# Attention with beacon keys into soft MoE: score banks of the next pair ahead of the extras, the turned dispatch weights two batches behind

## The chip, the cores and the metric

One core of one Trainium2 chip runs the whole program. The metric is the device time of one execution in microseconds, lower is better.

## The reference

Attention over 8 batches, 8 heads, 576 queries, width 64, with 16 beacon keys ahead of the 576 causal ones; its output, as 4608 tokens of width 512, goes into a soft mixture of 8 experts with 4 slots each. `a` is the attention weight matrix, `d` the dispatch weights (normalized over tokens), `c` the combine weights (normalized over slots).

```python
scores = scale * np.matmul(q, k_all.transpose(0, 1, 3, 2))      # causal mask, softmax -> a
attn = np.matmul(a, v_all)                                      # [8, 8, 576, 64]
x = attn.transpose(0, 2, 1, 3).reshape(4608, 512)
logits = x @ phi                                                # 32 slots
d = np.exp(logits - logits.max(0)); d /= d.sum(0) + 1e-09
slot_input = (d.T @ x).reshape(8, 4, 512)
for e in range(8):
    slot_out[e] = np.maximum(slot_input[e] @ w1[e], 0.0) @ w2[e]  # w1 512x1024, w2 1024x512
c = np.exp(logits - logits.max(1)); c /= c.sum(1) + 1e-09
out = c @ slot_out.reshape(32, 512)
```

## The kernel before

The order of the instructions on each engine (PE, DVE, ACT, POOL, and SP, which issues transfers) is the order of the Python calls. The work goes in 32 pairs of heads, n = 4b + g for batch b and g = 0 to 3; the main loop runs n = 2 to 31 and is one pair deep in a pipeline: iteration n makes the scores of pair n and the A.V product of pair n-1.

The steps that the loop calls, with the lines of the profile:

- `scores(n, bank)`: a quarter of pair n's causal scores, as PE matmuls (L517) into one of two PSUM score buffers ("sc"), the exponential of it on ACT (L522) into `expT` (two buffers, by pair), and the causal mask on POOL (L508). Bank 0 has 992 elements per partition, bank 1 928, bank 2 768, bank 3 640. A score buffer is free when its exponential has read it.
- `transposes(m, which)`: the k or q of two pairs turned on PE in two pieces (L486) and copied out by DVE (L498). In even iterations it is k, in odd ones q, always ahead of its use.
- `attend(n, hh)`: A.V of one head of the pair (L538), with a column of ones for the softmax sums; one PSUM buffer ("av") holds both heads.
- `normalize(n)`: DVE adds an epsilon to the sums (L549), inverts them (L551) and multiplies (L552) into the batch's `x`.
- `x_transposes(n)`: the pair's part of `x` turned (L564) and copied to `xT` by DVE (L571).

Once per batch there are four extras:

- `logits(b)`: `xT` times phi (L583), then its exponential on ACT (L589) into `dT`, each of the 32 slots four times over, 640 elements. The last batch does it in two steps (L592 on ACT for 160 elements, L593 on DVE for the three copies).
- `dispatch(b)`: `dT` against `x` (L622), the slot sums (L600), and their addition into `acc` on DVE (L633, L636).
- `combine_T(b)`: `dT` turned on PE (L644) and copied into `eT` by DVE (L647), for the output at the end.
- `cast_v` and `perm_v`: the next batch's values, cast on POOL (L390, L394), permuted on PE (L404) into one score buffer and two "tr" buffers, and copied out by ACT (L407) and DVE (L410).

The "tr" PSUM buffers are two. Each piece of the k or q transposes, each `x_transposes`, `logits`, `dispatch`, `combine_T`, and two pieces of `perm_v` take one in turn, so that each waits until the one before the last has been copied out. `x` has two buffers, so batch b writes where batch b-2 was; `dT` has one.

The weights (33.5 MB in f32) come in over the POOL queue in pieces of 512 KB of f16 (`load_weights`, L449 and L456), paced by the loop: none or one piece an iteration, then two from batch 6 on. The last ones are `wt`, of experts 6 and 7. q, k and v come in over the SP queue (L351, L365, L377, L381) up to two batches ahead.

After the loop come the last pair, the last batch's logits and dispatch, the two expert products (`first`, L823; `second`, L838), a normalization (L860), and the output: combine matmuls (L909), scaling on ACT and DVE (L914, L916) and 13 transfers (L920). `fill` (L658) is a matmul on constants whose result nobody reads.

Of the kernel before, what the change touches and what calls it, by code (L numbers as in the profile page):

```python
# [14 lines left out]
AF = mybir.ActivationFunctionType  # L15
# [253 lines left out]
def kernel(  # L269
# [12 lines left out]
    nc = tc.nc  # L282
    P = 128
    B, H, S, D = q.shape
    Nb = beacon_k.shape[2]
    E, Dm, F = moe_w1.shape
    NSL = moe_phi.shape[1]
# [5 lines left out]
    NC5 = 5  # L293
# [45 lines left out]
    def head(n, hh):  # L339

        g = n % NG
        return 2 * g + hh if n >= NPAIR - 2 else 4 * (g // 2) + 2 * hh + g % 2
# [126 lines left out]
    def transposes(m, which):  # L469

        b, hb = divmod(m, 2)
        t = st["kq"[which], b, hb]
        if which == 1:
            qTs[m] = work.tile([P, 2, S], BF, name="qT", tag="qT")
            dst = qTs[m][:, :, :]
        else:
            if m:
                beacon_keys(m)
            dst = kTs[m % 2][:, :, Nb:Nb + S]
        for j0, j1 in ((0, 5), (5, NJ)):  # L480
            tp = ps_tr.tile([P, j1 - j0, P], BF, name="trps", tag="tr")
            for j in range(j0, j1):
                for hh in range(2):
                    lo, hi = 64 * hh, 64 * hh + 64
                    if m < 2 * B - 1:
                        nc.tensor.transpose(tp[lo:hi, j - j0, :],  # L486
                                            t[:, hh, j, :].bitcast(BF)[:, 1::2], idb[:, :])
                        continue
                    for u in range(2):
                        nc.tensor.transpose(tp[lo:hi, j - j0, 64 * u:64 * u + 64],  # L490
                                            t[lo:hi, u, j, :].bitcast(BF)[:, 1::2],
                                            idb[lo:hi, lo:hi])
            do = dst.rearrange("p u (s j) -> p u s j", j=NJ)[:, :, :, j0:j1]
            ti = tp[:, :, :].rearrange("p j (u s) -> p u s j", u=2)
            if j0 and (m == 0 or m == 1 and which):
                nc.scalar.activation(do, ti, AF.Copy)
            else:
                nc.vector.tensor_copy(out=do, in_=ti)  # L498
# [12 lines left out]
    def scores(n, bank, masked=True):  # L511
        base, w, mms = BANKS[bank]
        sc = ps_sc.tile([P, 2, 512], FP, name="sc", tag="sc")
        for (c, q0, qw, col) in mms:
            for hh in range(2):
                po = 64 * hh
                nc.tensor.matmul(sc[:, hh, col:col + qw],  # L517
                                 kTs[n // 2 % 2][po:po + D, n % 2, c * P:(c + 1) * P],
                                 qTs[n // 2][po:po + D, n % 2, q0:q0 + qw], start=True,
                                 stop=True)  # L520
        ex = exps[n % 2]
        nc.scalar.activation(ex[:, :, base:base + w], sc[:, :, 0:w], AF.Exp, scale=scale)  # L522
        if masked:
            select(n, bank)
# [3 lines left out]
    def attend(n, hh):  # L528
        b, g = divmod(n, NG)
        h = head(n, hh)  # L530
        if hh == 0:
            pool, tag = (ps_av, "av") if n < NPAIR - 1 else (ps_sc, "sc")
            avs[n] = pool.tile([P, 2, 512], FP, name="av", tag=tag)
        av = avs[n][:, hh, 0:NC5 * DD].rearrange("p (i d) -> p i d", d=DD)
        for i in range(NC5):
            for c in range(i + 1):
                o = BLK[c, i]
                nc.tensor.matmul(av[:, i, :], exps[n % 2][0:KW[c], hh, o:o + P],  # L538
                                 vhs[b % 2][0:KW[c], c, h, :],
                                 start=(c == 0), stop=(c == i))  # L540
# [17 lines left out]
    dTs = {}  # L558

    def x_transposes(n):  # L560
        b, t = divmod(n, NG)
        tp = ps_tr.tile([P, S], F16, name="xtps", tag="tr")
        for i in range(NC5):
            nc.tensor.transpose(tp[:, QLO[i]:QLO[i] + QW[i]],  # L564
                                xs[b][0:QW[i], i, 2 * t:2 * t + 2, :].rearrange(
                                    "p h d -> p (h d)"),
                                idh[0:QW[i], 0:QW[i]])
        if n == NPAIR - 2:
            nc.scalar.activation(xT[:, t, 0:S], tp[:, :], AF.Copy)
        else:  # L570
            nc.vector.tensor_copy(out=xT[:, t, 0:S], in_=tp[:, :])  # L571
# [3 lines left out]
    def logits(b, t0=0, t1=NDC):  # L575

        if t0 == 0:
            lps[b] = ps_tr.tile([P, NC5, NSL], FP, name="lgps", tag="tr")
            dTs[b] = work.tile([P, NC5, 4, NSL], F16, name="dT", tag="dT", bufs=1)
        lp = lps[b]  # L580
        for i in range(NC5):
            for t in range(t0, t1):
                nc.tensor.matmul(lp[:, i, :], xT[:, t, QLO[i]:QLO[i] + P],  # L583
                                 phih[:, t, :], start=(i == 0 and t == 0),
                                 stop=(i == NC5 - 1 and t == NDC - 1))
        if t1 < NDC:
            return
        if t0 == 0:
            nc.scalar.activation(dTs[b][:, :, :, :],  # L589
                                 lp[:, :, :].unsqueeze(2).broadcast_to([P, NC5, 4, NSL]), AF.Exp)  # L590
        else:
            nc.scalar.activation(dTs[b][:, :, 0, :], lp[:, :, :], AF.Exp)  # L592
            nc.vector.tensor_copy(  # L593
                out=dTs[b][:, :, 1:4, :],
                in_=dTs[b][:, :, 0:1, :].broadcast_to([P, NC5, 3, NSL]))

    def slot_sums(b, sp, into):
        for i in range(NC5):
# [40 lines left out]
    def combine_T(b):  # L639

        dT = dTs[b]
        tp = ps_tr.tile([P, S], F16, name="etps", tag="tr")
        for i in range(NC5):
            nc.tensor.transpose(tp[:, QLO[i]:QLO[i] + QW[i]],  # L644
                                dT[0:QW[i], i, :, :].rearrange("p g s -> p (g s)"),
                                idh[0:QW[i], 0:QW[i]])
        nc.vector.tensor_copy(out=eT[:, b * S:(b + 1) * S], in_=tp[:, :])  # L647
# [5 lines left out]
    def fill(count, late=True):  # L653

        pool, tag = (ps_tr, "tr") if late else (ps_av, "av")
        ps = pool.tile([P, 512], FP, name="fill", tag=tag)
        for _ in range(count):
            nc.tensor.matmul(ps[:, :], onesh[:, :], eT[:, 0:512], start=True, stop=True)  # L658
# [14 lines left out]
    with tc.manual_schedule(engines={ET.PE, ET.DVE, ET.Activation, ET.Pool, ET.SP}):  # L673
# [3 lines left out]
                          in_=beacon_k.rearrange("b h n d -> (b h) (n d)"))  # L677
# [44 lines left out]
        for c in range(4):  # L722
            for t in range(4):
                nc.vector.tensor_copy(
                    out=sel[32 * c:32 * c + 32, t, :].rearrange(
                        "p (m t) -> p m t", t=4)[:, :, t],
                    in_=idh[32 * c:32 * c + 32, 32 * c:32 * c + 32])
# [22 lines left out]
        load_v(2)  # L750
        load_qk(2, 0)

        for n in range(2, NPAIR):
            b, g = divmod(n, NG)
            scores(n, 0)
            scores(n, 1)
            if n // 2 + 1 < 2 * B:
                transposes(n // 2 + 1, n % 2)
            attend(n - 1, 0)
            scores(n, 2)  # L760
            if n >= 3:
                x_transposes(n - 3)
            attend(n - 1, 1)
            if n >= 7 and g == 3:
                combine_T(b - 1)
            normalize(n - 1)
            scores(n, 3)
            if n == NPAIR - 1:
                x_transposes(n - 2)
            if b and g == 2:  # L770
                logits(b - 1)
            if n >= 8 and g == 0:
                dispatch(b - 2)
            if b + 1 < B and g:
                parts = ((0,), (1,), (2,))[g - 1] if b else ((0,), (1, 2))[g - 2]
                for c in parts:
                    cast_v(b + 1, c)
                if g == 3:
                    perm_v(b + 1)
            if b + 2 < B:  # L780
                if g == 0:
                    load_v(b + 2)
                    load_qk(b + 2, 0)
                if g == 2:
                    load_bv(b + 2)
                    load_vr(b + 2)
                    load_qk(b + 2, 1)
            if n == 5:
                nc.vector.tensor_copy(out=phih[:, :, :], in_=phif[:, :, :])
            load_weights((0, 1, 1, 1)[g] if b < 6 else 2)  # L790
# [6 lines left out]
        n = NPAIR  # L797
# [3 lines left out]
        normalize(n - 1)  # L801
        x_transposes(n - 2)
        dispatch(B - 2)
        fill(2)
        x_transposes(n - 1)
        logits(B - 1, 0, NDC - 1)
        logits(B - 1, NDC - 1, NDC)
# [3 lines left out]
            out=sz1[:, :].rearrange("p (t e s) -> p t e s", t=NDC, s=SPE), in_=sizv)  # L811
# [148 lines left out]
```

## Time and profile before

| | |
|---|---|
| three runs | 201.41, 202.38, 203.35 us; median 202.38 |
| profiled execution | 200.63 us, its span 198.9 us, mean granted clock 0.956 |
| busy PE / DVE / ACT / POOL | 162.4 / 132.4 / 134.0 / 114.8 us |
| exponentials of scores (L522) | 128, 104.8 us |
| matmuls of scores (L517) and of A.V (L538) | 576 and 960, 43.7 and 40.3 us |
| DMA moved | 55.90 MB, 281 GB/s over the span |

The first 22 us fill the pipeline, the loop runs to about 153 us, the experts to 169 us, and the output to the end. PE is the busiest engine by its own time, but busy time is an average over all of these; the DMA rows give the share of the core's 16 DMA engines in use. A form such as `128x640` is partitions by elements. Times in the timeline count from the start of the span.

### The profile page before, as it was taken

How to read it: one execution, taken by the hardware profiler on the slowest of the kernel's cores; microseconds unless marked ns; L12 is line 12 of the kernel's file. 1: busy time of each engine (PE TensorE's matmuls, PEld its weight loads, DVE VectorE, ACT ScalarE, POOL GpSimd, SP SyncE). 2: the span in 40 equal slices, each digit the busy share in tenths (PEclk: the TensorE clock that was granted, in tenths of full speed). 3: DMA queues.
4: the chain of work that ended last, by engine and by line, in shares of the span. 5: the costliest groups of instructions: out<-in, count | busy, mean ns of one | idle time of the engine just before them, and what ended most of it. 6: DMA issues, size and time to landing. Idle time of an engine off the chain costs nothing.

```text
span 198.9 us, 7368 instructions
## 1 busy us (share of the span) xinstructions
PE 162.4 (82%) x3122; PEld 107.9 (54%) x3122; DVE 132.4 (67%) x279; ACT 134.0 (67%) x172; POOL 114.8 (58%) x264
## 2 busy tenths in 40 slices
PE   6798893889898898988989898898978999875200
PEld 2443561667586576756757665675856844542000
DVE  0352684678888888888789778788855532898300
ACT  2356694688888889888888788888787140783200
POOL 6049087359659847955965786799776400890000
PEclk9999999699999999999999999999999999997855
DMA  6999999999999999999999999999999995599991
GB/s 203 258 240 367 283 357 326 264 377 316 280 242 379 279 258 326 319 258 292 381 249 270 363 305 269 257 229 211 216 211 214 214 213 95 211 410 415 409 403 69
DMA packets 29845, 55.90 MB, mean 281 GB/s; under 512 B 7244, under 2 KB 15660, under 8 KB 29804
## 3 DMA queue, kind: packets, MB, share of 16 engines
q1 hardware_dynamic: 24764, 37.98, 56.0%
q0 software_dynamic: 4752, 16.78, 42.3%
q10 hardware_dynamic: 288, 0.59, 1.0%
q8 instruction: 26, 0.43, 0.8%
q14 instruction: 15, 0.12, 0.2%
HBM read 62.69 MB, written 9.44 MB: 363 GB/s over the span
## 4 chain that ended last, share of the span: by engine, by line


## 5 line engine op out<-in xcount | busy, mean ns | idle before, releaser
L522 ACT ACTIVATE expT<-sc 128x992 f16<-128x992 f32 (+3 forms) x128 | 104.8, 867 | 20.3 <-PE sc L517 19.7
L508 POOL TENSOR_SCALAR_AFFINE_SELECT expT<-expT 128x224 f16<-128x224 f16 (+3 forms) x128 | 55.1, 441 | 39.6 <-ACT expT L522 38.7
L517 PE MATMUL sc<-qT,kT 64*128 64x80 bf16 (+4 forms) x576 | 43.7, 246 | 11.2 <-ACT expT L522 5.4
L538 PE MATMUL av<-vh,expT 128*128 128x65 f16 (+1 forms) x960 | 40.3, 195 | 0.2 <-DVE x L552 0.2
L538 PEld LDWEIGHTS <-expT 128*128 128x128 f16 (+1 forms) x960 | 33.6, 98 | 4.3 <-POOL expT L508 0.8
L498 DVE COPY kT<-trps 128x640 bf16<-128x640 bf16 (+1 forms) x31 | 22.7, 773 | 19.6 <-PE trps L486 19.1
L517 PEld LDWEIGHTS <-kT 64*128 64x128 bf16 x576 | 17.1, 95 | 28.2 <-issue 22.4
L498 DVE COPY qT<-trps 128x640 bf16<-128x640 bf16 (+1 forms) x30 | 22.0, 773 | 8.4 <-PE trps L486 6.6
L552 DVE TENSOR_TENSOR x<-av,r 128x640 f16<-128x640 f32 x32 | 26.4, 824 | 1.1
L390 POOL CAST vc<-vstag 128x512 f16<-128x512 f32 x32 | 18.7, 614 | 1.6 <-ACT expT L522 1.6
L571 DVE COPY xT<-xtps 128x576 f16<-128x576 f16 x31 | 14.1, 456 | 6.0 <-PE xtps L564 5.8
L914 ACT ACTIVATE osb<-fps,rc 128x512 f32<-128x512 f32 (+1 forms) x18 | 11.2, 675 | 10.2 <-PE fps L909 9.5
L564 PE MATMUL xtps<-idh,x 128*128 128x128 f16 (+2 forms) x160 | 14.3, 217 | 0.4 <-issue 0.2
L916 DVE TENSOR_SCALAR osb<-fps,rc 128x512 f32<-128x512 f32 (+1 forms) x19 | 12.8, 727 | 1.3 <-PE fps L909 1.2
L658 PE MATMUL fill<-eT,onesh 128*128 128x512 f16 x36 | 11.6, 451 | 1.7 <-POOL onesh L691 1.5
L407 ACT ACTIVATE vh<-vps 128x1024 f16<-128x1024 f32 x8 | 8.2, 1027 | 6.6 <-PE vpt L404 6.6
L410 DVE CAST vh<-vpt 128x512 f16<-128x512 f32 x16 | 10.3, 684 | 3.6 <-PE vpt L404 3.6
L564 PEld LDWEIGHTS <-x 128*128 128x128 f16 (+2 forms) x160 | 9.2, 98 | 6.0 <-issue 5.5
L909 PE MATMUL fps<-so,eT 128*128 128x512 f16 (+1 forms) x37 | 11.2, 431 | 1.2 <-DVE so L860 0.8
L465 POOL COPY kT<-bkA 64x32 bf16<-64x32 bf16 x32 | 7.4, 232 | 7.9 <-DVE bkA L719 7.0
L486 PE MATMUL trps<-idb,kstag 128*64 128x128 bf16 x270 | 11.7, 234 | 0.1
L486 PE MATMUL trps<-idb,qstag 128*64 128x128 bf16 x270 | 10.9, 222 | 0.7 <-DVE vh L410 0.4
(98 smaller groups left out, 187.6 us busy)
## 6 DMA issues: line engine op xcount, KB each, us to landing
kstag<-in_k_dram SPq DMA_DIRECT2D x15, 576.0 KB, 10.0
qstag<-in_q_dram SPq DMA_DIRECT2D x15, 576.0 KB, 13.6
out_dram<-osb SPq DMA_DIRECT2D x11, 768.0 KB, 7.2
vstag<-in_v_dram SPq DMA_DIRECT2D x7, 1024.0 KB, 14.8
w1h<-in_moe_w_dram POOLq DMA_DIRECT2D x10, 512.0 KB, 8.6
w2h<-in_moe_w_dram POOLq DMA_DIRECT2D x10, 512.0 KB, 8.4
wt<-in_moe_w_dram POOLq DMA_DIRECT2D x7, 512.0 KB, 12.2
wv<-in_moe_w_dram POOLq DMA_DIRECT2D x4, 512.0 KB, 11.6
```

Of the source, the lines that this page charges most:

```text
L390: nc.gpsimd.tensor_copy(out=st["c", b][:, :, hs, :].rearrange("p t h d -> p h t d"), in_=st["v", b][:, hs, :, :])
L486: nc.tensor.transpose(tp[lo:hi, j - j0, :], t[:, hh, j, :].bitcast(BF)[:, 1::2], idb[:, :])
L498: nc.vector.tensor_copy(out=do, in_=ti)
L508: nc.gpsimd.affine_select(out=ap, in_=ap, compare_op=AL.is_ge, fill=0.0, base=cbase, pattern=pat, channel_multiplier=-1)
L517: nc.tensor.matmul(sc[:, hh, col:col + qw], kTs[n // 2 % 2][po:po + D, n % 2, c * P:(c + 1) * P], qTs[n // 2][po:po + D, n % 2, q0:q0 + qw ...
L522: nc.scalar.activation(ex[:, :, base:base + w], sc[:, :, 0:w], AF.Exp, scale=scale)
L538: nc.tensor.matmul(av[:, i, :], exps[n % 2][0:KW[c], hh, o:o + P], vhs[b % 2][0:KW[c], c, h, :], start=(c == 0), stop=(c == i))
L552: nc.vector.tensor_tensor(out=xs[b][:, :, head(n, 0):head(n, 1) + 1:head(n, 1) - head(n, 0), :].rearrange("p i h d -> p h i d"), in0=av[:, ...
L564: nc.tensor.transpose(tp[:, QLO[i]:QLO[i] + QW[i]], xs[b][0:QW[i], i, 2 * t:2 * t + 2, :].rearrange("p h d -> p (h d)"), idh[0:QW[i], 0:QW ...
L571: nc.vector.tensor_copy(out=xT[:, t, 0:S], in_=tp[:, :])
L658: nc.tensor.matmul(ps[:, :], onesh[:, :], eT[:, 0:512], start=True, stop=True)
L916: nc.vector.tensor_scalar(out=ou, in0=f[:, 0:hw], scalar1=rc[:, bb, j:j + 1], scalar2=None, op0=AL.mult)
```

## The change

Five things change, all in the order of calls but for one:

1. The exponential of the logits is always done in two steps: ACT writes 160 elements and DVE makes the three copies.
2. `scores(n + 1, 0)` is called in iteration n, after `normalize(n - 1)` and ahead of that iteration's extra, and `scores(2, 0)` ahead of the loop.
3. `scores(n, 2)` is called ahead of `attend(n - 1, 0)`, and `scores(n, 3)` ahead of `attend(n - 1, 1)`.
4. `combine_T` of batch b-2 is called at g = 0 after the normalization (it was that of batch b-1 at g = 3, ahead of the normalization), and that of batch 6 in the tail, where it takes the place of two fills.
5. `dispatch` of batch b-2 is called at g = 1 (it was g = 0).

The expression for the parts of `cast_v` is written in another way and gives the same parts.

```diff
@@ logits
-        if t0 == 0:
-            nc.scalar.activation(dTs[b][:, :, :, :],
-                                 lp[:, :, :].unsqueeze(2).broadcast_to([P, NC5, 4, NSL]), AF.Exp)
-        else:
-            nc.scalar.activation(dTs[b][:, :, 0, :], lp[:, :, :], AF.Exp)
-            nc.vector.tensor_copy(
-                out=dTs[b][:, :, 1:4, :],
-                in_=dTs[b][:, :, 0:1, :].broadcast_to([P, NC5, 3, NSL]))
+        nc.scalar.activation(dTs[b][:, :, 0, :], lp[:, :, :], AF.Exp)
+        nc.vector.tensor_copy(
+            out=dTs[b][:, :, 1:4, :],
+            in_=dTs[b][:, :, 0:1, :].broadcast_to([P, NC5, 3, NSL]))
@@ the main loop
+        scores(2, 0)
         for n in range(2, NPAIR):
             b, g = divmod(n, NG)
-            scores(n, 0)
             scores(n, 1)
             if n // 2 + 1 < 2 * B:
                 transposes(n // 2 + 1, n % 2)
+            scores(n, 2)
             attend(n - 1, 0)
-            scores(n, 2)
             if n >= 3:
                 x_transposes(n - 3)
+            scores(n, 3)
             attend(n - 1, 1)
-            if n >= 7 and g == 3:
-                combine_T(b - 1)
             normalize(n - 1)
-            scores(n, 3)
             if n == NPAIR - 1:
                 x_transposes(n - 2)
+            else:
+                scores(n + 1, 0)
+
+            if b > 1 and g == 0:
+                combine_T(b - 2)
+            if b > 1 and g == 1:
+                dispatch(b - 2)
             if b and g == 2:
                 logits(b - 1)
-            if n >= 8 and g == 0:
-                dispatch(b - 2)
             if b + 1 < B and g:
-                parts = ((0,), (1,), (2,))[g - 1] if b else ((0,), (1, 2))[g - 2]
-                for c in parts:
+                for c in ((g - 1,) if b else ((), (0,), (1, 2))[g - 1]):
                     cast_v(b + 1, c)
                 if g == 3:
                     perm_v(b + 1)
@@ the tail
         dispatch(B - 2)
-        fill(2)
+        combine_T(B - 2)
         x_transposes(n - 1)
```

## The prediction

> **What bounds the kernel now.** I read the page's DMA rows first, then the busy times by stretch, then the landing of the last weights, then one pair of heads in the timeline.
>
> ```profile
> DMA  6999999999999999999999999999999995599991
> ```
>
> ```profile
> core 0: us, PE busy (x) PEld busy (x) DVE busy (x) ACT busy (x) POOL busy (x), PEclk, DMA share, GB/s
> 62.00:79.00 17.00, 15.88 (x355) 11.40 (x356) 14.36 (x30) 14.56 (x19) 12.22 (x29) 1.00 1.07 300
> 135.00:152.00 17.00, 14.82 (x357) 10.61 (x354) 11.41 (x25) 14.39 (x19) 13.15 (x30) 1.00 1.06 213
> 152.00:165.00 13.00, 12.49 (x244) 8.22 (x241) 6.71 (x22) 4.36 (x8) 3.50 (x7) 1.00 1.05 210
> 171.00:195.00 24.00, 10.61 (x50) 5.19 (x48) 13.91 (x28) 10.18 (x17) 7.55 (x9) 0.79 0.98 393
> ```
>
> Two things compete. The DMA engines are full (share 1.05 to 1.07) through the loop up to 165 us, and again (0.98) while the output is written. The 300 and 213 GB/s are no sign of room: weights are halved on the way in, from f32 to f16, so 213 moved is 426 read, and the loop mixes them with q, k and v. In a loop batch TensorE and VectorE are nearly full too (15.88 and 14.36 of 17.00 us). The end tells which comes last. The last two weight pieces are issued by 154.39:
>
> ```profile
> wt<-in_moe_w_dram POOLq DMA_DIRECT2D x2, 256.0 KB, 13.4
> ```
>
> That row, from the DMA view of 154.3 to 155.0, holds both (median time to landing); the first alone takes 13.0, so the second takes about 13.8 and lands at 168.1 us. Its reader is the end of the second expert product:
>
> ```profile
> 167.36 0.38 PE L838 MATMUL so<-wt,hT 128*32 128x512 f16 x2
> 167.58 0.38 PE L838 MATMUL so<-wt,hT 128*32 128x512 f16 x2
> 167.79 0.77 PE L838 MATMUL so<-wt,hT 128*32 128x512 f16 x2
> 168.20 0.58 PE L838 MATMUL so<-wt,hT 128*32 128x512 f16 x2
> ```
>
> The groups follow each other at 0.21 to 0.22 us, the last at 0.41: TensorE waited some 0.2 us for that landing. So the weights set the end, and the compute is only 0.2 us ahead of them. Everything later (the output, 168.1 to 198.9) is left as it is.
>
> The loop that the change reorders looks like this (TensorE, iteration n=10):
>
> ```profile
> 76.29 0.39 PE L517 MATMUL sc<-qT,kT 64*128 64x496 bf16 x2
> 77.19 0.38 PE L517 MATMUL sc<-qT,kT 64*128 64x384 bf16 x4 [0.51 <-ACT expT L522]
> 77.49 0.69 PE L486 MATMUL trps<-idb,kstag 128*64 128x128 bf16 x18
> 78.12 0.64 PE L538 MATMUL av<-vh,expT 128*128 128x65 f16 x15
> 78.69 0.34 PE L517 MATMUL sc<-qT,kT 64*128 64x128 bf16 x4
> 78.96 0.43 PE L564 MATMUL xtps<-idh,x 112*128 112x112 f16 x5
> 79.23 0.62 PE L538 MATMUL av<-vh,expT 128*128 128x65 f16 x15
> 79.78 0.32 PE L517 MATMUL sc<-qT,kT 64*128 64x80 bf16 x8
> ```
>
> Bank 1 waits 0.51 us because the two score buffers are taken: it needs the exponential of the previous pair's bank 3. The cycle is bank 3 to its exponential 0.42, exponential 0.70, release 0.06, then on TensorE 0.30 + 0.63 + 0.57 + 0.27 + 0.27 + 0.55 = 2.59: together 3.77. L552 starts 3.76 and 3.77 us apart in plain iterations, 4.39 with the logits, 4.79 with the value permutation: 16.71 a batch.
>
> **The change part by part.** *Exponentials of the logits.* ACT does 160 elements instead of 640 (L592's 304 ns for L589's 697), seven times: 2.8 us less on ACT. VectorE gets seven copies of L593's form, 308 ns each: 2.2 us more. One step is longer, since sums and turned weights need the copy, but both are now a batch later.
>
> *Scores ahead.* Bank 3 goes ahead of the second A.V (0.57) and the next bank 0 ahead of the extra. The exponential of bank 3 is then done about when bank 1 wants it, and the cycle above is broken. What takes its place in a plain iteration: A.V 0.57, bank 0 to its exponential 0.49, exponential and release 1.06, bank 2 0.27, A.V 0.57, x transposes 0.23, bank 3 0.25: 3.44, a gain of 0.32.
>
> *The extras.* All share the two small PSUM buffers ("tr") with the transposes. Before, an extra's result left its buffer at once: L647 (eT) ran ahead of the normalization, L589 ahead of the next bank-0 exponential. Now each eviction is queued behind one of these, and the second half of the next k or q transposes waits for that buffer. After that wait TensorE needs 0.27 + 0.27 + 0.57 + 0.23 + 0.25 = 1.59 to the next second A.V. Counted from one second A.V to the next:
> - Turned weights: to L549 0.69, L549 and L551 0.45, L552 0.82 less 0.09 overlap, eT 0.46 and release 0.05: 2.38 + 1.59 = 3.97.
> - Dispatch: the normalization writes x into the buffer that dispatch of two batches back still reads, and dispatch now stands behind it. L552 waits: A.V 0.57, bank 0 0.22, dispatch 0.71 (L622's 0.67 and the hand-over), L552 0.73, acc 0.28 + 0.05: 2.56 + 1.59 = 4.15. Behind L552 on VectorE wait acc and the k copies; TensorE waits for acc.
> - Logits: 0.57 + 0.49 + 0.90 (exponential of bank 0) + 0.36 (the short one): 2.32 + 1.59 = 3.91, against 4.39.
> - Values: the matmuls wait for the bank-3 exponential, 0.93 after the A.V, take 1.08, then two casts, 0.59 and 0.73: 3.33 + 1.59 = 4.92, against 4.79.
>
> Sum 16.95 a batch against 16.71: 0.24 slower. For n=3 to 8, with few extras, the gain is 3 x 0.32 + 0.48 (logits), less 0.13 (values) and about 0.3 at n=4, where the late value cast, already waited for, now also stands behind a select: 1.0 us net. Five full batches give back 1.2. In the last three iterations, by the same steps, dispatch and turned weights cost some 0.4 more. In the tail TensorE gets from the second A.V of pair 30 to the first of pair 31 in 0.57 + 0.23 + 0.43 = 1.23 us where the trace has 1.89 (weight loads at 151.33 and 153.22), 0.6 less; the turned weights (0.38) replace two fills (0.4), and their eT copy holds the logits 0.1. Sum: -1.0 + 1.2 + 0.4 - 0.5 = +0.1 us on the compute's arrival.
>
> The unknown is the hand-overs: some dozen a batch are new on the path, each known to 0.03 to 0.05 us. Over six batches that is 2.2 to 3.6 us to the bad side. To the good side, if all late evictions were hidden, each extra would cost only itself: four times 3.44 plus logits' 0.36 and values' 1.0 is 15.1 a batch, 10 us in the loop. I take the middle of the near part, +0.1 to +1.5. The weights don't follow either way: their bytes are the same and the engines are full before and after, so they land at 168.1 less at most the idle part of one gap (21.00 to 23.50, share 0.90 against 1.07: 0.4 us), which lies ahead of the loop. An early arrival only waits. The end moves by 0 to 1.5 less the 0.2 margin; I take +0.4. The profiled execution is 200.63 (198.9 span and 1.7 around it) and would be 201.0; the median shown is 202.38, so 202.8.
>
> One rule speaks against the change. The trace's clock was 0.50 in 34.70:38.10, after 2.1 us without a matmul (30.50:32.60, waiting for the cast of values); bank 1 to the second A.V took 3.38 there against 2.04 at 77.19. The Trainium skill, "TensorE: Matmul & The Clock Gate", Part 1, says that about 3.4 us of idle halves the clock; the trace has it after a shorter pause. By that rule an early TensorE that waits for weights would run its last product and first output matmuls at half speed: an estimate of 1 us from L838's 0.38 and L909's 0.59 us, each doubled, still within 1%. By the rows it arrives too late to idle so long.
>
> **Rivals.**
> - *Slower: late evictions on the tr buffers.* For it: three of the four extras now have theirs behind other work, and L552 behind dispatch holds VectorE itself. Against: all durations are from rows. Hand-overs 0.05 longer than I took: 0.1 + 3.6 - 0.2 is 3.5 us, so 205.9. It decides from 0.2 us of late arrival, since the compute has no more margin.
> - *Faster: the waits for exponentials were the time.* For it: ACT waits 13.4 us for scores between 45 and 150. With 15.1 a batch the compute would be 10 us early, 192.4, if the weights came as early. Against: the share of 1.05 to 1.07 from 45 to 165 leaves no room; cut by the DMA it is 202.0, no change.
> - *It does nothing.* The order of matmuls changes, but the score wait is replaced by the buffer wait in each iteration with an extra: 202.4. That is close to the forecast, and shares its chance.
>
> **How the numbers follow.** No change, within 1% (2 us; about what a measurement of this kernel can tell from none, as its runs lie 201.4 to 203.4): 0.58. Slower by over 1%: 0.34, the first rival from half its price on. Faster by over 1%: 0.08, mostly that the DMA share misleads. The range starts at 200.8, the DMA's 0.6 us and the fast side of the runs, and ends at 206.3, the slower rival with its upper hand-overs.
>
> **What would show it.** Right: DMA share again 1.05 or more up to 165; last weights within 0.5 us of 168.1; L838's last group waiting longer or the same; bank 1's wait for ACT gone from plain iterations (3.4 us), and transposes (L486) waiting for eT, acc and the short exponential; L552 waiting for dispatch once a batch from n=9. Batches near 17 us. Wrong: the last weights over 1 us earlier, or the second product ending well after they have landed.

## The result, and the profile after

The changed kernel takes 202.82 us (median of 20 runs, 201.68 to 205.69); the kernel before, run beside it, 202.79 (20 runs, 201.15 to 205.18). The ratio is 1.0048, 95% interval 1.0025 to 1.0070; it comes from undisturbed runs compared round by round, so it is not the quotient of the two medians. So a loss of about 0.5% is measured, inside the 1% that was called no change. The profiled execution took 203.55, its span 201.8, mean clock 0.949.

The DMA row of the page, the busy times in the stretches that the prediction shows (columns as there), and the last two weight pieces (DMA view, 155 to 156 us):

```profile
DMA  6999999999999999999999999999999993699990
```

```profile
62.00:79.00 17.00, 15.74 (x339) 11.04 (x335) 13.78 (x30) 14.33 (x18) 11.44 (x28) 1.00 1.07 295
135.00:152.00 17.00, 15.72 (x370) 11.34 (x366) 12.97 (x28) 14.80 (x21) 13.38 (x31) 1.00 1.06 213
152.00:165.00 13.00, 12.68 (x272) 9.24 (x272) 7.21 (x23) 5.33 (x9) 4.97 (x10) 1.00 1.06 213
171.00:195.00 24.00, 10.97 (x56) 6.06 (x55) 14.91 (x30) 10.84 (x18) 8.87 (x9) 0.78 0.92 369
```

```profile
wt<-in_moe_w_dram POOLq DMA_DIRECT2D x2, 256.0 KB, 14.4
```

The DMA engines are as full as before up to 165 us (1.06, 1.07). The last piece is issued at 155.19 and lands at 169.95; it was 154.39 and 168.14. (The last stretch falls a little earlier in the output than before, since all is later.) The end of the second expert product, from the timeline of TensorE; L836 is the old L838, as lines from L589 on are four lower:

```profile
168.71 0.38 PE L836 MATMUL so<-wt,hT 128*32 128x512 f16 x1 [0.20 <-DMA wt<-in_moe_w_dram]
...
169.99 0.38 PE L836 MATMUL so<-wt,hT 128*32 128x512 f16 x1 [0.67 <-DMA wt<-in_moe_w_dram]
```

TensorE now waits visibly for the weights, 0.20 and then 0.67 us. The first expert product, before and after:

```profile
158.98 1.91 PE L823 MATMUL hps<-w1h,siz 128*32 128x512 f16 x32
```

```profile
159.74 1.91 PE L821 MATMUL hps<-w1h,siz 128*32 128x512 f16 x32
```

The compute came 0.8 us later, the weights 1.8 us later, so the weights still set the end in this execution. The two profiles are single executions: the one before (200.63) is below all of the 20 runs above, 2.2 us under their median, the one after 0.7 us over the median of its own. So their 2.9 us of span is more than the 0.5% that the runs show, and differences of a microsecond between the two need the runs beside them.

The loop, TensorE with turned weights and then dispatch:

```profile
73.23 0.47 PE L486 MATMUL trps<-idb,qstag 128*64 128x128 bf16 x10
74.05 0.41 PE L486 MATMUL trps<-idb,qstag 128*64 128x128 bf16 x8 [0.35 <-DVE eT L643]
74.40 0.34 PE L517 MATMUL sc<-qT,kT 64*128 64x128 bf16 x4
74.67 0.63 PE L538 MATMUL av<-vh,expT 128*128 128x65 f16 x15
75.14 0.42 PE L564 MATMUL xtps<-idh,x 112*128 112x112 f16 x5
75.49 0.32 PE L517 MATMUL sc<-qT,kT 64*128 64x80 bf16 x8
75.74 0.63 PE L538 MATMUL av<-vh,expT 128*128 128x65 f16 x15
...
78.40 0.41 PE L486 MATMUL trps<-idb,kstag 128*64 128x128 bf16 x8 [0.30 <-DVE acc L632]
```

And the waits of 45 to 150 us (in total, times, longest):

```profile
DVE x L552 <- PE sips L618: 3.0, 6, 0.5
...
DVE dT L589 <- ACT dT L588: 2.0, 6, 0.3
PE trps L486 <- DVE eT L643: 1.7, 5, 0.4
...
PE trps L486 <- DVE vh L410: 1.6, 5, 0.3
...
PE trps L486 <- DVE acc L632: 1.2, 4, 0.3
```

The score wait of the old L517 (0.51 us in most iterations) is gone from the list. In its place the second piece of the k or q transposes waits for a "tr" buffer, 0.3 to 0.4 us in the iterations with turned weights, dispatch and values; for the logits no such wait is listed, but the 18 transposes there take 0.93 us (at 81.88), where the kernel before has 0.71 (at 81.26). The normalization waits 0.5 us for dispatch once a batch. Starts of L552: 3.44 and 3.47 us apart in plain iterations, and 4.51, 3.90, 4.03, 5.09 in a full batch: 17.53 us against 16.71.

### The profile page after: what moved, and what is told of

Read it like the earlier page. It is cut to its first block, busy times and chain, and to the rows that moved or that the text cites. A ratio compares the mean times of both kernels' runs of the same rounds, so it can differ in the third digit from the quotient of the medians.

```text
span 201.8 us, 7383 instructions
## 1 busy us (share of the span) xinstructions
PE 164.5 (82%) x3120; PEld 109.7 (54%) x3120; DVE 133.5 (66%) x286; ACT 134.0 (66%) x172; POOL 114.3 (57%) x264
## 4 chain that ended last, share of the span: by engine, by line
## 5 line engine op out<-in xcount | busy, mean ns | idle before, releaser
L522 ACT ACTIVATE expT<-sc 128x992 f16<-128x992 f32 (+3 forms) x128 | 108.0, 864 | 22.8 <-PE sc L517 19.4
L517 PE MATMUL sc<-qT,kT 64*128 64x80 bf16 (+4 forms) x576 | 45.3, 246 | 2.1 <-ACT expT L522 0.9
L538 PEld LDWEIGHTS <-expT 128*128 128x128 f16 (+1 forms) x960 | 33.0, 98 | 7.1 <-issue 4.7
L552 DVE TENSOR_TENSOR x<-av,r 128x640 f16<-128x640 f32 x32 | 26.4, 825 | 3.9 <-PE sips L618 3.0
L517 PEld LDWEIGHTS <-kT 64*128 64x128 bf16 x576 | 17.7, 95 | 16.9 <-issue 7.6
L486 PE MATMUL trps<-idb,kstag 128*64 128x128 bf16 x270 | 13.6, 233 | 4.2 <-DVE vh L410 2.1
L486 PEld LDWEIGHTS <-kstag 128*64 128x64 bf16 x270 | 10.2, 116 | 9.0 <-issue 8.7
L486 PE MATMUL trps<-idb,qstag 128*64 128x128 bf16 x270 | 12.7, 223 | 2.9 <-DVE eT L643 1.7
L564 PE MATMUL xtps<-idh,x 128*128 128x128 f16 (+2 forms) x160 | 13.6, 216 | 0.2 <-DVE acc L632 0.2
L549 DVE TENSOR_SCALAR stat<-av 128x10 f32<-128x10 f32 x32 | 5.4, 169 | 11.6 <-PE av L538 11.6
L486 PEld LDWEIGHTS <-qstag 128*64 128x64 bf16 x270 | 9.1, 109 | 7.1 <-issue 6.9
L654 PE MATMUL fill<-eT,onesh 128*128 128x512 f16 x34 | 11.0, 456 | 1.5 <-POOL onesh L687 1.5
## 6 DMA issues: line engine op xcount, KB each, us to landing
wt<-in_moe_w_dram POOLq DMA_DIRECT2D x7, 512.0 KB, 11.3
```

Source lines behind the costliest of these rows:

```text
L486: nc.tensor.transpose(tp[lo:hi, j - j0, :], t[:, hh, j, :].bitcast(BF)[:, 1::2], idb[:, :])
L517: nc.tensor.matmul(sc[:, hh, col:col + qw], kTs[n // 2 % 2][po:po + D, n % 2, c * P:(c + 1) * P], qTs[n // 2][po:po + D, n % 2, q0:q0 + qw ...
L552: nc.vector.tensor_tensor(out=xs[b][:, :, head(n, 0):head(n, 1) + 1:head(n, 1) - head(n, 0), :].rearrange("p i h d -> p h i d"), in0=av[:, ...
L564: nc.tensor.transpose(tp[:, QLO[i]:QLO[i] + QW[i]], xs[b][0:QW[i], i, 2 * t:2 * t + 2, :].rearrange("p h d -> p (h d)"), idh[0:QW[i], 0:QW ...
```

## The experiments

Where not said otherwise, an edit is made to the changed kernel. "Interval" is the time between two starts of L552, "first product" the start of the first expert matmul.

**Half of the weights away, before and after.** Experts 4 to 7 use the weights of 0 to 3, so that the DMA engines have nothing to do from some 130 us on.

```diff
-    NRES = 5
+    NRES = 4
...
-    wchunks = [(e, m, j) for es_ in ((0, 1, 2, 3), (4,)) for m in range(2)
+    wchunks = [(e, m, j) for es_ in ((0, 1, 2, 3),) for m in range(2)
                for e in es_ for j in range(2)]
-    wchunks += [(e, 0, j) for e in (5, 6, 7) for j in range(2)]
-    wchunks += [(e, 1, j) for j in range(2) for e in (5, 6, 7)]
@@ weight
+        e = e % NRES
```

> The kernel before, but experts 4 to 7 use the weights of experts 0 to 3 and theirs are not loaded (16 of 32 pieces left out; the output is that of other weights). The compute is the same, only the transfers are fewer. Theory (weights land last, the compute is 0.2 us ahead of them): between 0.2 and 1.5 us faster than before, since a typical run may have its weights later than the profiled one. Rival (the compute in the loop is itself slowed by the full DMA engines): several us faster, with loop batches shorter than 16.7 us.

> The changed kernel with the same half of the weights left out. Now only the compute sets the end. Theory: it is slower than the light kernel before by the compute's late arrival, 0.8 us by the first expert product (159.74 against 158.98 us in the two profiles), 0.4 to 1.2. Rival (the small loss of the change comes from later weights, not from the compute): no slower than the light kernel before.

Measured beside 202.04 for the kernel before: light_before 201.92, ratio 0.9979 (0.9944 to 1.0014); light_after 202.00, ratio 0.9961 (0.9924 to 0.9998). Two things follow. Before the change, half of the weights cost almost nothing (0.4 us by the ratio, at the low end of the 0.2 to 1.5 expected, and not told from none): the compute alone takes as long, so the end was a tie and not the DMA's alone. And with the weights gone the changed kernel is not measurably slower, although its batches are 17.53 against 16.71. The 0.4 to 1.2 us that were expected as the compute's own loss don't show, so this pair speaks for the rival, that the small loss comes with the weights. The full weights cost the kernel before 0.2% (1 against 0.9979) and the changed one 0.9% (1.0048 against 0.9961); the intervals of these two differences overlap a little, so that the weights took more of the loss than the compute did is likely, not shown.

**The value permutation left out from batch 2 on**, with all loads kept, once with all weights and once with half of them.

```diff
     def perm_v(b):
+        if b > 1:
+            return
```

> The changed kernel without the value permutation from batch 2 on (its matmuls and copies are left out and A.V reads older values; all loads and casts stay). Six iterations of 5.1 us become about 3.5, so the compute is 8 to 10 us early. Theory (weights set the end): no change beyond 1 us, the last weights land where they did, and the second expert product waits many us for them. Rival (the compute sets the end): 8 to 10 us faster.

> Both cuts at once: the changed kernel without the value permutation from batch 2 on and with half of the weights. Theory: now the saved compute shows, 8 to 10 us faster than the light kernel after. Rival (something else than weights and this compute, such as the loads of q, k and v, paces the loop): less than 4 us faster than the light kernel after.

Measured: noperm_light 195.56, ratio 0.9675 (0.9627 to 0.9724), 6.4 us less than light_after, between the 8 to 10 of the theory and the rival's "less than 4". noperm_after 206.35, ratio 1.0197 (1.0127 to 1.0266): with the same early loop but all of the weights, it is slower than the kernel before and the changed one. No theory on record had that. In its timeline and its waits (100 to 150 us):

```profile
132.48 1.17 PE L488 MATMUL trps<-idb,kstag 128*64 128x128 bf16 x18 [7.02 <-DMA kstag<-in_k_dram]
```

```profile
POOL vc L390 <- DMA vstag<-in_beacon_v_dram: 13.0, 2, 9.7
```

TensorE ran out of k (7.02 us), and POOL stood 9.7 us at the cast of the next values. Behind that cast, on the same queue, are the weights: one piece was issued at 122.60 and the next at 136.81. They land until 174.18.

**Dispatch and turned weights in each other's place; then also an earlier value cast in batch 1; that with half of the weights; and a third buffer for x.**

```diff
-            if b > 1 and g == 0:
-                combine_T(b - 2)
-            if b > 1 and g == 1:
-                dispatch(b - 2)
+            if b > 1 and g == 0:
+                dispatch(b - 2)
+            if b > 1 and g == 1:
+                combine_T(b - 2)
@@ swap_cast and l_swap_cast only
-                for c in ((g - 1,) if b else ((), (0,), (1, 2))[g - 1]):
+                for c in ((g - 1,) if b else ((), (0, 1), (2,))[g - 1]):
@@ l_x3 only (half of the weights, order of the changed kernel)
-            xs[b] = work.tile([P, NC5, H, D], F16, name="x", tag="x")
+            xs[b] = work.tile([P, NC5, H, D], F16, name="x", tag="x", bufs=3)
   (and bufs=3 at the two other tiles with tag="x")
```

> The changed kernel with the two extras exchanged: dispatch of batch b-2 at g = 0 and its turned weights at g = 1. The multiplication into x (L552) no longer finds dispatch still reading its buffer. Theory (late evictions on the tr buffers, of which the wait of L552 for dispatch is one): batch 17.53 us to 17.0 to 17.1, some 2.5 us less compute, but the weights set the end, so the time falls by 0.3 to 1 us against the changed kernel. Rival (the wait of L552 is idle time off the path): batch stays at 17.5.

> The same, and the second half of batch 1's value cast at n = 2 instead of n = 3, where TensorE sat 2.7 us waiting for it and fell to half clock at 34 us. Theory: that iteration goes from 8.8 to 5 to 6 us with no half clock, so the compute is 5 to 6 us ahead of that of the changed kernel; the weights hold the end, so 1 to 2 us faster than the changed kernel at most, and the second product waits for them. Rival (the compute sets the end): 5 us faster.

> The same two edits with half of the weights left out (experts 4 to 7 use those of 0 to 3). Nothing but the compute sets the end: 5 to 6 us faster than the light kernel of the changed one (about 196.5 us). If the compute's gain were not real, or eaten by waits for q and k, less than 3.

> The changed kernel with half of the weights left out, and three buffers for x instead of two, so that L552 never waits for dispatch; all else is as changed. For the intervals between L552s alone. Theory: the one with turned weights and dispatch falls from 4.51 by 0.3 to 0.5, the batch from 17.53 to about 17.1; the eviction of the turned weights still costs. Rival (the wait is off the path): no shorter batch.

Measured beside 202.47 for the kernel before: swap 202.08, ratio 1.0025 (0.9983 to 1.0066), batch 3.89 + 4.06 + 4.03 + 5.09 = 17.07. l_x3 201.29 (one run), batch 4.05 + 3.90 + 4.03 + 5.09 = 17.07. So dispatch's hold on x is 0.46 us of the batch, by both ways. In the time it is not told from nothing: the ratio is 0.2% below that of the changed kernel, and the two intervals overlap.

l_swap_cast 198.46, ratio 0.9862 (0.9795 to 0.9930): the early cast takes the one long interval from 8.78 to 5.51. By the ratios the kernel takes 2.0 us less than light_after (by the medians, of two sessions, 3.5), where 5 to 6 were expected and "less than 3" stood for a gain eaten by waits. The profile shows these: the first product starts at 157.12, only 2.2 us ahead of light_after's 159.32, as four of the iterations with the logits take 4.65 to 5.16 us and not 4.03. Ahead of each of them POOL's cast waits for the values, so that POOL's masks come late and the A.V product waits for these (the waits of 45 to 130 us, where light_after has no such row, and one such product):

```profile
POOL vc L390 <- DMA vstag<-in_beacon_v_dram: 8.5, 5, 2.4
```

```profile
80.55 0.52 PE L537 MATMUL av<-vh,expT 128*128 128x65 f16 x10 [0.92 <-POOL expT L507]
```

swap_cast, the same with all weights, 208.29, ratio 1.0320 (1.0263 to 1.0376): slower again. Its profiled execution took 210.15, more than the other five; what is read from it here, starved TensorE and late values, stands in the profiles of noperm_after and sc_ahead too. The queue that issues k, q and v (SP), waits from 95 to 130 us, first of the kernel before, then of swap_cast:

```profile
SPq L381 <- DMA vstag<-in_v_dram: 11.1, 2, 5.6
```

```profile
SPq L381 <- DMA vstag<-in_v_dram: 19.9, 2, 11.9
```

L381 brings the beacon rows into the tile that L365 fills, so it waits until L365 has landed, and the next k and q stand behind it in SP's queue. That landing takes longer here: the last k and q are issued at 127.71 and 128.53, not at 117.16 and 117.72, though TensorE is earlier. Then POOL waits for the same values:

```profile
136.89 1.17 POOL L390 CAST vc<-vstag 128x512 f16<-128x512 f32 x2 [7.48 <-DMA vstag<-in_beacon_v_dram]
138.00 0.55 POOL L456 DMA_DIRECT2D w2h<-in_moe_w_dram  x1
```

The weights ahead of 138.00 were issued by 126.02, and in 135 to 140 the DMA share falls to 0.79. The last weights land at 174.85, but they don't set this end: TensorE waits 1.05 us for k and 2.39 us for q, the first product starts only at 166.15, and the last matmuls of the second expert product start at 177.83.

**Three ways to issue the weights in swap_cast**, and the scores alone.

```diff
@@ swap_cast has, at the end of an iteration
             load_weights((0, 1, 1, 1)[g] if b < 6 else 2)
@@ sc_pace
+            load_weights((0, 1, 0 if b in (4, 5) else 1, 1)[g] if b < 7 else 4)
@@ sc_mid
+            load_weights((0, 1, 0 if b in (4, 5) else 1, 1)[g] if b < 6 else 2)
@@ sc_ahead: the line of swap_cast, ahead of the value cast
@@ l_order: light_before, with scores(n, 2), scores(n, 3), scores(n + 1, 0) and scores(2, 0)
   placed as in the change, and nothing else of it
```

> The same as swap_cast, but fewer weight pieces are issued while k, q and v still come: 2 a batch in batches 4 and 5 (not 3), 3 in batch 6 (not 8), 4 an iteration in batch 7. Theory (weights crowd out the loads of k, q and v on full DMA engines, TensorE then starves and POOL's own wait holds the later weights back): the 11 us interval between two normalizations near the end is gone (none over 6.5 us), the last k, q and v are issued before 120 us (126.9 in swap_cast), the last weights land at 167.5 to 170, and the time is 201.5 to 203.5, ratio 0.995 to 1.01. Rival (compute that comes early simply runs into loads that can't come sooner, whatever the weights do): an interval over 8 us stays and the time is 206 or more, ratio 1.02 or more.

> The same as swap_cast, but in each iteration the weights are issued ahead of the value cast on POOL, so that a cast that waits for v does not hold up that iteration's weights. Theory (crowding by weights is the cause, the blocked queue only a part): the interval of some 11 us stays, the DMA engines' idle time of 1.4 us between 120 and 140 goes or halves, the time is 206 to 208. Rival (the blocked POOL queue is the whole loss): DMA share stays at 1.03 or more up to 165 us, last weights land by 170, and the time is 202 to 204.

> The kernel before with half of the weights left out (experts 4 to 7 use those of 0 to 3), and of the change only the order of the scores: bank 3 ahead of the second A.V, next bank 0 ahead of the extra. Turned weights, dispatch and the wide exponential of the logits stay where they were. By the steps of the prediction: plain iterations 3.44, dispatch 3.9, logits 4.3 to 4.5, values with turned weights 5.3 to 5.6, a batch 17.0 to 17.4: the move of turned weights and dispatch costs next to nothing, and the loss of the batch belongs to the scores. Rival (the moved extras are what makes the batch long): logits 4.1, values with turned weights at most 4.9, a batch of 16.2 or less.

> Between swap_cast and sc_pace: 2 weight pieces a batch in batches 4 and 5, but 2 an iteration again from batch 6 on, that is from some 120 us, after the last loads of k, q and v have been issued (119.4 in sc_pace). Theory (the loads and the weights share full DMA engines, so nothing may crowd out k, q and v before 120 us, and nothing may leave the engines idle after it): no interval between two normalizations over 6.5 us, DMA share 1.03 or more from 45 to 165 us (sc_pace fell to 0.61 and 0.77 in stretches of 5 us), last weights at 168.5 to 171, 202.0 to 204.5 us, ratio 1.00 to 1.015: most of the 3% of swap_cast comes back, nothing is gained on the kernel before, because the bytes are the same. Rival (a compute that is 3 us early can't be fed by any issue order of the weights): a starved interval of over 8 us or an idle stretch of the DMA engines stays, last weights at 172 or later, 206 or more, ratio 1.02 or more.

Measured beside 202.32: sc_ahead 210.21, ratio 1.0362 (1.0267 to 1.0458). The idle time of the DMA engines in 120 to 140 went, as expected, but TensorE starved again (7.03 us for k, one interval of 12.35), and the time is above all that was expected. Here too the compute ends last: the weights land at 173.66, and the second product's last matmuls start at 176.75. So the blocked POOL queue is not the whole loss, and putting weights first makes the starving no better.

sc_pace 213.04, ratio 1.0532 (1.0479 to 1.0585). The first half of its theory held: no interval up to the last pair is over 5.50, and the last k and q are issued at 118.40 and 119.44. The second half did not: too many weights were held back. The rival's time came (206 or more) without its sign, as no interval is over 8 us. Its stretches, DMA share in the column before the last, and the last pair in the timeline:

```profile
125.00:130.00 5.00, 4.87 (x106) 3.49 (x103) 4.45 (x9) 4.03 (x6) 3.44 (x8) 1.00 0.61 152
130.00:135.00 5.00, 4.96 (x112) 3.49 (x112) 3.84 (x10) 4.34 (x7) 4.68 (x12) 1.00 0.86 121
135.00:140.00 5.00, 4.47 (x116) 3.08 (x105) 4.31 (x9) 4.22 (x6) 3.24 (x9) 1.00 0.82 146
140.00:145.00 5.00, 4.51 (x123) 3.41 (x118) 4.27 (x9) 4.51 (x6) 3.97 (x10) 1.00 0.77 125
```

```profile
156.03 0.35 PE L538 MATMUL av<-vh,expT 128*128 128x65 f16 x3 [4.98 <-POOL expT L508]
```

The share lost in these 20 us, against 1.06, is 5 x (0.45 + 0.20 + 0.24 + 0.29) = 5.9 us of transfer, about half of what is missing at the end: the last weights land at 179.44, 11.3 us later than in the kernel before. And the burst of issues held POOL. In the trace the weight pieces signal eight semaphores of the program in turn, and an issue waits until the piece eight before it has landed: landings at 154.73, 157.19 and 159.64 are followed by issues at 155.01, 157.47 and 159.93. The masks of the last pair stood behind such issues, so that TensorE waited 4.98 us for them.

sc_mid, beside 201.74: 205.80, ratio 1.0190 (1.0145 to 1.0235), above the 202.0 to 204.5 expected and just under the rival's 206. Neither theory is right as it stood. TensorE doesn't starve (longest interval after the start 5.11), the DMA engines are at 1.05 to 1.11 in each 5 us from 110 to 165, the first product starts at 157.05, 1.9 us ahead of the kernel before; and the last weights still land at 172.15:

```profile
169.69 0.51 PE L836 MATMUL so<-wt,hT 128*32 128x512 f16 x1 [2.09 <-DMA wt<-in_moe_w_dram]
170.93 0.59 PE L836 MATMUL so<-wt,hT 128*32 128x512 f16 x1 [0.73 <-DMA wt<-in_moe_w_dram]
```

Here are full engines and no starving, and still the weights land 4.0 us later. What grew is the time of the transfers themselves. The DMA view from 0 to 165 us has the queue of k, q and v with all of its packets (count, MB, share of the 16 engines' time), in the kernel before, the changed kernel and sc_mid:

```profile
q1 hardware_dynamic: 22892, 28.54, 53.4%
```

```profile
q1 hardware_dynamic: 22892, 28.54, 54.0%
```

```profile
q1 hardware_dynamic: 22892, 28.54, 56.1%
```

The same packets and bytes take 88.1, 89.1 and 92.6 us of all engines: 1.0 and 4.5 more. Most of it is the 2304-byte packets of k and q, at 102.6, 105.0 and 109.1 ns; the weights' own packets stay at 325 to 327.

l_order 202.6 (one run; beside 202.32): intervals 3.89, 3.45, 5.00, 4.89, a batch of 17.23, in the range of the first theory. Its terms lie elsewhere than its text had them: logits 5.00 for 4.3 to 4.5, values 4.89 for 5.3 to 5.6, because the copy of the turned weights stands ahead of the normalization that ends the logits' interval. Of the 0.82 us by which the batch grew, the order of the scores alone makes 0.52, and the rest, which the theory had at next to nothing, adds 0.30.

## Why the prediction was right, and where it was not

- **No change, at 202.8:** right. The reason given, weights that land last with the compute 0.2 us ahead of them, fits the profile, and light_before shows how close the two were. That the DMA engines stay full up to 165 us and L836 waits longer for its weights came as written.
- **The plain iteration** (3.44): 3.43 to 3.47. **The waits that take the score wait's place** came at eT, at acc and at the values' copies, and at L552 for dispatch, as the sums have them; the wait for the short exponential, named as a sign, is not in the list.
- **A batch of 16.95:** too small, 17.53. From one second A.V to the next: turned weights 4.06 (for 3.97), dispatch 4.36 (4.15), logits 4.03 (3.91), values 5.08 (4.92). The term that was mis-sized most is the end part that all four share: 74.05 to 75.74 is 1.69, not 1.59, since the delayed piece takes 0.35 (not 0.27), and the A.V product and the x transposes 0.82 (not 0.80). That is 0.4 of the 0.58; 0.1 is dispatch, which starts 0.32 after bank 0, not 0.22. Over six batches 0.58 is 3.5 us: in the batches the hand-overs came at their bad bound.
- **+0.1 us on the compute's arrival:** +0.8, within the range of +0.1 to +1.5, but of terms that were off both ways, so that the sum is in part luck. The intervals of n=3 to 8 gained 1.0 as forecast, though the logits gained 0.34 (not 0.48), the value permutation lost 0.30 (not 0.13), and n=4 lost nothing (not 0.3); the iteration ahead of them cost 0.2. The five batches lost 2.9, not 1.2; it would have been 4.1, but the kernel before had 1.6 us of irregular pauses in them (one lengthens the interval from 114.57 by 0.35; the profile names only TensorE's own issue for it), the changed kernel 0.3. The last iterations and the tail gained 1.3 where 0.1 was forecast. In the time it shows even less: with half of the weights the changed kernel is 0.9961, not over 1.
- **"The weights don't follow either way, they land at 168.1":** this step failed. They landed at 169.95 in the profile, and the runs with full weights lost more than those with half. Bytes and shares were the same, but a share says only that the engines are busy: the packets of k, q and v took 1.0 us more of it. In swap, where they took 53.8% of 165 us (88.8 us), the last weights landed at 168.52. Whether the change causes this 1.0 us is not shown: in the profiles of the seven kernels without an early loop the same packets take 88.1 to 90.2 us, and the kernel before has the least.
- **"An early arrival only waits":** this failed most clearly, though the forecast did not rest on it. A lead of some microseconds made the kernel 2 to 3% slower (noperm_after, swap_cast), where the same edits with half of the weights made it 1.4 to 3.3% faster. An early TensorE frees buffers and asks for k, q and v sooner; they and the weights share full engines, the values' second load holds SP's queue, and POOL, which also issues the weights, stops at the cast, so that with all weights TensorE can starve. The sign they share: from 45 to 150 us POOL's cast waits for the values 3 to 5 times (5.5 to 15.1 us) in each of the seven kernels with an early loop, and never in the other seven. Holding back the weights (sc_mid) ended the starving; that it was the weights which crowded out the loads is thereby likely, and that the time still grew shows that it wasn't all.
- **The rivals.** Slower (205.9 through hand-overs): its mechanism was there (the late evictions cost 0.82 us a batch), but the compute came only 0.8 us later, not 3.7. Faster: the batch never came near 15.1. The 202.0 for a fast compute "cut by the DMA" was too hopeful: with all weights such kernels took 205.8 to 213.0.
- **The clock.** In the changed kernel the last product did not run at half speed: 0.38 us at 169.99. In sc_mid, after a wait of 2.09 us, L836's matmuls took 0.51 and then 0.59 (the lines above), and the granted clock of 170 to 172 us was 0.50. The Trainium skill, "TensorE: Matmul & The Clock Gate", Part 1, has the clock halve after about 3.4 us of idle. In sc_mid the wait began at some 167.6, the clock was 0.90 in 169 to 170 and 0.50 from 170 on, so it had halved at most 2.4 us after the last matmul: earlier than the Trainium skill has it.

What stays open: why k and q packets take longer in kernels whose compute is early. All seven kernels with an early loop (the two noperm, swap_cast, l_swap_cast and the three sc kernels) have them at 107.3 to 109.3 ns on average, all others at 102.6 to 106.3; each is one execution. The traces narrow it down: from 20 us on, 2919 of these packets in sc_mid start with value packets but no weight packet in flight and take 115.0 ns, in the kernel before 2153 that take 103.0; with neither beside them it is 103.3 against 99.6. So it is mostly where k, q and the values are loaded at once, and why that takes longer stays open. Issuing k and q ahead of the values' second load, so that SP's queue is not held, was not tried. No version here that computes the same result beats the kernel before.

## What to carry to other kernels

When the engines and the DMA finish within a microsecond of each other, as here, a change to the one is worth little until the other is moved too. A kernel with half of its bytes, and one with part of its compute left out, tell which case it is. Being early is not free: ask which loads an early engine will trigger, what they share engines with, and what else is issued from the queue that will wait for them. A DMA share of 1.06 says that the engines are busy, not that they move the same bytes per microsecond; compare one queue's packets, bytes and share between two profiles.

## What the runs showed of the hardware

- The time of a DMA packet of one size is not fixed: 2304-byte loads took 102.6 to 109.3 ns on average from one kernel to the next, 4096-byte casting weight loads 324.7 to 335.1. Over 7936 packets of k and q that is 3.3 us of all 16 engines.
- With only weights in flight (140 to 160 us), the kernel before, the changed one and sc_mid all read 422 GB/s of f32 (211 written as f16, of the 214 that the windows show): there they are alike, and the differences arise while k, q and v are loaded.
- An issue that waits for an earlier piece holds its whole engine: in sc_pace POOL's issues came 2.4 us apart from 150 us on, each 0.28 or 0.29 us after the landing that its semaphore stood for, and the masks behind them were late.
